# Doubling a decay table on ScalarE, issuing the last output rows from two queues, and moving TensorE's filler work, in a kernel of sliding attention and a long convolution

## The chip, the cores and the metric

One core of one Trainium2 chip. The metric is the device time of one execution in microseconds (us), lower is better. The engines have short names in the profile: PE is TensorE's matmul, PEld its weight load, DVE is VectorE, ACT is ScalarE, POOL is GpSimd, SP is SyncE, which here only issues transfers. A name with a q (SPq, ACTq, POOLq) is the instruction queue of that engine.

## The reference

Two independent heads stand side by side in the output: columns 0 to 639 come from A, columns 640 to 1279 from B.

```python
# A: sliding attention, 32 heads of 20, 8 taps at distance 2
qkv = x @ wqkv                              # (2048, 640) @ (640, 1920)
idx = pos[:, None] - arange(8) * 2          # key positions of each query
logits = einsum("bhsd,bhswd->bhsw", q, k[idx]) * Dh ** -0.5   # -1e9 where idx < 0
attn = softmax(logits, axis=-1)
o = einsum("bhsw,bhswd->bhsd", attn, v[idx])
a = o.transpose(...).reshape(B, S, D) @ wo

# B: diagonal state space layer as a causal convolution of length 2048
logdA = exp(log_dt)[:, None] * (A_re + 1j * A_im)             # (640, 192)
P = exp(logdA[:, :, None] * arange(L))
K = einsum("dn,dnl,dn->dl", Cc, P, dB).real                   # kernel of each channel
y = irfft(rfft(pad(u)) * rfft(pad(K)))[:L] + u * Dskip
return concatenate([a, b], axis=-1)
```

## The kernel before

**The first half builds the convolution kernels, in five chunks of channels** (`c` = 0 to 4 in `body`, line 851). The powers `exp(logdA * l)` are not computed one by one: for each chunk `exps_chunk` (line 236) makes a table `R` of real exponentials with ScalarE, `phase_table` (line 267) makes sines from products of TensorE (tables `TA` and `TX`), and VectorE multiplies them into a left factor X (`small_half`, line 310) and a right factor Y (`y_form`, line 341). TensorE sums X times Y over the states (`kgen_unit`, line 351, tile `ps_k`). VectorE's order in this half is PG, X, Q, X and then the Y products of each unit, chunk after chunk. The Fourier steps of the earlier chunk (`fwd`, lines 369 to 388, with ScalarE evicting `ps_f`) and the product of u with the skip factor (`times_d`, line 436) lie between.

**Exponentials with two multipliers at once.** `exps_chunk` can make the rows for multipliers m and 2m with one instruction if it finds alpha and 2 alpha side by side. So for every chunk but the first it writes 2 alpha into the place of the alpha of the chunk before (`twice`, lines 246 to 250), which may happen only when the exponentials of the chunk before have read it. In the kernel before, GpSimd makes this sum of two float32 tiles of 128x192 (line 248). GpSimd's queue also carries the two fills of the table with ones (lines 244 and 245) and the ten stores of `times_d` (line 442). The tile UD that `times_d` writes has one buffer, so VectorE can write the next UD (line 441) only when the store of the last one has landed.

**The second half is attention and the way back from the Fourier domain.** After the projections of q, k and v the loop over `GROUPS` (line 984) takes steps n = 0 to 47, eight for each of six groups of query columns. A step (`av_step`, line 666) is one VectorE product of v with the attention weights into a ring of six buffers, and 16 small matmuls of 32 rows by 32 columns that add it up in `ps_o`; after the eighth step ScalarE evicts `ps_o`. Steps of VectorE, TensorE and ScalarE are kept in the order of the program in this half (`in_order`, line 970), so that where a piece of work stands in the loop is where its engine does it.

**Fillers.** Between the steps the dictionary `FILLS` (line 982) puts pieces of other work: `(r, p)` at step n takes r pieces of the output projection (`out_piece`, line 707) and p pieces of the inverse transform of B (`part`, line 757, 12 or so matmuls of 96 rows into `ps_ib` and an eviction by ScalarE to `ysb`; 24 pieces in all). In group 0 the fillers of a step stand ahead of its `av_step`, in the other groups behind it. The softmax of the second half of the columns runs inside the loop: maximum and difference at n = 2, the exponential with its one ScalarE instruction at n = 3 (line 990), the sums over the eight taps by TensorE (`sums`, line 628, two taps at each of n = 8, 10, 12 and 14, tile `ps_x`), the reciprocal and the product by VectorE at n = 17.

**The end.** `out_piece` is called 16 times. It multiplies a block of attention output with wo (`ps_op` or `ps_x`), evicts it to one of six `ob` tiles by ScalarE (in the last two pieces ScalarE one half, VectorE the other) and stores it in 1, 2 or 4 transfers. The pieces count themselves in `nop`; from the twelfth on (`late`, line 713) all their transfers, 16 in number, are issued by SP.

Of the kernel before, what the change touches and what calls it, by code (L numbers as in the profile page):

```python
# [10 lines left out]
A = mybir.AluOpType  # L11
# [224 lines left out]
def exps_chunk(tc, pools, B, c):  # L236
    nc = tc.nc
    flat = pools["tab"].tile([128, 9216], bf16, name="R", tag=f"R{c % 2}")
    RA = flat[:, 0:3072].rearrange("p (h g q a f) -> p h g q a f", h=2, g=2, a=8, f=4)
    RX = flat[:, 3072:9216].rearrange("p (q e f) -> p q e f", e=32, f=4)  # L240
    al = B["alpha"][:, c]
    by_half = al.rearrange("p (h v) (q f) -> p h (v q) f", h=2, f=4)
    src = al.rearrange("p u (q f) -> p (u q) f", f=4)
    nc.gpsimd.memset(flat[:, 0:3072].rearrange("p (x a f) -> p x a f", a=8, f=4)[:, :, 0, :], 1.0)
    nc.gpsimd.memset(RX[:, :, 31, :], 1.0)
    if c > 0:
        twice = B["alpha"][:, c - 1]
        nc.gpsimd.tensor_tensor(out=twice, in0=al, in1=al, op=A.add)  # L248
        both = B["alpha"][:, c - 1:c + 1]
        both = both.rearrange("p e u (q f) -> p (u q) e f", f=4)  # L250
    exp = lambda o, i, m: nc.scalar.activation(out=o, in_=i, func=ACT.Exp, scale=m)  # L251
# [12 lines left out]
    return RA, RX  # L264
# [190 lines left out]
class Attention:  # L455
# [251 lines left out]
    def out_piece(self, rows, last=False):  # L707
# [17 lines left out]
        if whole:  # L725
            self.copy(out=ob.rearrange("p (h n) -> p h n", h=2), in_=ps)
        for k in range(ns):
            (nc.gpsimd, nc.sync)[late or k % 2].dma_start(out=self.out_a[512 * (s0 + k) + i0:512 * (s0 + k) + i0 + ni, :], in_=ob[ni * k:ni * k + ni])
# [50 lines left out]
def body(tc, ctx, pools, prm, B_u, B_Dskip, Sd, Zd, UDd, A_x, A_wqkv, A_wo, out_a, out_b):  # L779
    nc = tc.nc  # L780
# [193 lines left out]
    def fill(some, n=1):  # L974
        for f in some[0:n]:
            f()
        del some[0:n]
# [4 lines left out]
    FILLS = {1: (0, 2), 3: (0, 2), 5: (0, 1), 7: (0, 1), 9: (0, 1), 11: (0, 2), 13: (0, 2), 15: (0, 1), 17: (1, 0), 19: (2, 2), 23: (1, 2), 27: (2, 2), 31: (2, 2), 35: (2, 2), 37: (0, 2), 39: (1, 0), 43: (1, 0), 45: (1, 0)}  # L982
    LOADS = {(2, 8)[n // NCH] + n % NCH: (2 + n // NCH, n % NCH) for n in range(2 * NCH)}
    for group, (i0, ni, j0, nj, done) in enumerate(GROUPS):
        for w in range(W):
            n = 8 * group + w
            if group == 0:
                fill(parts, FILLS.get(n, (0, 0))[1])
                if w == 3:
                    att.exp(1)  # L990
                if w in (0, 3):
                    att.proj_v(16 + 2 * (w == 3))
                if w == 5:
                    att.v_halo(8, 12)
# [83 lines left out]
```

## Time and profile before

| | us |
|---|---|
| median of 3 runs | 424.67 |
| the 3 runs | 406.79, 424.67, 425.53 |
| the profiled execution, own time | 407.56 |
| its span, first to last instruction | 405.8 |
| HBM traffic in it | 19.69 MB read, 14.16 MB written |

The profile is a page of one execution. Its views: the busy time of each engine; the chain of waits followed back from the last instruction; groups of instructions by line with their durations; and, asked for a stretch, the timeline of one engine, in which a row gives start, length, engine, line, operation, out<-in, count, and in brackets the idle time before it with what ended it. A view by stretches gives each engine's busy time and the clock that TensorE was granted (1.00 is full speed). An engine that is not the bound may idle for free; what counts is the engine that is busy all through a stage, and which wait ends last there.

### The profile page before, as it was taken

To read this page: it belongs to the slowest core of one execution; us is meant where nothing else is said; L and a number is where in the kernel's file an instruction comes from. 1 tells how busy PE (TensorE), PEld (TensorE's weight loads), DVE (VectorE), ACT (ScalarE), POOL (GpSimd) and SP (SyncE) were. 2 spreads that over 40 slices of the span, in tenths; PEclk is the share of its full clock that TensorE was granted. 3 is DMA by queue.
4 is the path that set the end of the run, shared out by engine and by line. 5 is a ranking of instruction groups with operands and counts; after the bars stand their busy time and mean duration, and the time that the engine had idled before them with its cause. 6 is when DMAs were issued, how large, how long until landed. Compare 5 with 4: busy or idle time off the path is not lost.

```text
span 405.8 us, 18754 instructions
## 1 busy us (share of the span) xinstructions
PE 349.7 (86%) x8565; PEld 260.6 (64%) x8565; DVE 370.3 (91%) x350; ACT 307.9 (76%) x532; POOL 100.6 (25%) x114
## 2 busy tenths in 40 slices
PE   1279779979898789889988989999999999899994
PEld 0267667878786679768787666656755676335652
DVE  7999999999989999999799999997967899889961
ACT  2996999879999999989999576533778544845662
POOL 8771049000101000399801000100020030302220
PEclk9999989989989999988999999999999999958998
DMA  5599102132044002420039655301652264797542
GB/s 143 155 235 193 22 4 107 57 81 56 29 151 115 3 3 81 135 55 2 31 112 152 124 93 133 100 4 24 214 162 79 104 160 107 209 254 222 163 125 74
DMA packets 40839, 43.36 MB, mean 107 GB/s; under 512 B 24144, under 2 KB 34288, under 8 KB 40120
## 3 DMA queue, kind: packets, MB, share of 16 engines
q1 hardware_dynamic: 35960, 30.60, 31.3%
q0 software_dynamic: 4656, 11.44, 9.3%
q8 instruction: 67, 1.10, 1.1%
q10 hardware_dynamic: 144, 0.12, 0.1%
q14 instruction: 12, 0.10, 0.1%
HBM read 19.69 MB, written 14.16 MB: 83 GB/s over the span
## 4 chain that ended last, share of the span: by engine, by line
PE 38%; ACT 21%; DVE 18%; issue 15%; DMA 3%; POOL 2%; SPq 1%; ACTq 0%; DVEq 0%; POOLq 0%
ACT R L251 8%; DVE X L317 6%; DVE Y L347 5%; PE ps_q L556 5%; PE ps_k L538 4%; PE ps_v L569 4%; DVE PG L317 3%; PE ps_x L472 3%; PE ps_o L472 3%; PE ps_op L472 3%; ACT A L380 3%; PE ps_ph L288 3%; PE ps_k L360 2%; POOL LPB L248 2%; DVE Q L317 2%
## 5 line engine op out<-in xcount | busy, mean ns | idle before, releaser
L347 DVE TENSOR_TENSOR Y<-PG 128x3072 bf16<-128x3072 bf16 x60 | 103.0, 1754 | 4.1 <-PE ps_k L365 4.1
L251 ACT ACTIVATE R<-LPB 128x192 bf16<-128x192 f32 (+1 forms) x185 | 56.5, 409 | 0.6 <-POOL LPB L248 0.5
L360 PE MATMUL ps_k<-Y,X 128*32 128x64 bf16 x1920 | 46.3, 239 | 10.3 <-DVE Y L347 9.5
L248 POOL TENSOR_TENSOR LPB<-LPB 128x192 f32<-128x192 f32 x4 | 45.9, 11470 | 29.4 <-ACT R L251 25.8
L288 PE MATMUL ps_ph<-LPB,LPA 128*64 128x256 bf16 x320 | 35.1, 323 | 12.7 <-DMA LPA<-lo 7.8
L360 PEld LDWEIGHTS <-X 128*32 128x32 bf16 x1920 | 32.8, 117 | 19.7 <-issue 8.9
L387 ACT CAST A<-ps_f 128x1024 bf16<-128x1024 f32 x40 | 37.6, 1036 | 7.4 <-PE ps_f L386 7.4
L365 PE MATMUL ps_k<-Y,X 64*32 64x64 bf16 x1920 | 42.9, 233 | 0.0
L380 ACT CAST A<-ps_f 128x1024 bf16<-128x1024 f32 x40 | 37.7, 1041 | 0.6 <-PE ps_f L379 0.6
L317 DVE TENSOR_TENSOR X<-R,TX 128x1536 bf16<-128x1536 bf16 x40 | 37.7, 963 | 0.3 <-DMA LPA<-hi 0.3
L386 PE MATMUL ps_f<-A,T 128*64 128x128 bf16 x640 | 29.1, 258 | 8.5 <-ACT A L380 8.4
L365 PEld LDWEIGHTS <-X 64*32 64x32 bf16 x1920 | 29.5, 112 | 8.6 <-issue 0.9
L386 PEld LDWEIGHTS <-T 128*64 128x64 bf16 x640 | 27.1, 129 | 10.1 <-issue 9.1
L679 DVE TENSOR_TENSOR prod<-v,atp 128x1536 bf16<-128x1536 bf16 (+3 forms) x32 | 30.9, 1023 | 2.4 <-PE ps_o L472 1.2
L296 ACT ACTIVATE TX<-ps_ph 128x768 bf16<-128x768 int16 x40 | 30.0, 836 | 1.1 <-PE ps_ph L292 1.0
L296 ACT ACTIVATE TA<-ps_ph 128x768 bf16<-128x768 int16 x40 | 29.7, 815 | 0.5 <-PE ps_ph L292 0.2
L288 PEld LDWEIGHTS <-LPA 128*64 128x64 bf16 x320 | 18.3, 124 | 17.0 <-DMA LPA<-hi 7.9
L589 DVE TENSOR_TENSOR prod<-qT,kT 128x1024 bf16<-128x1024 bf16 (+1 forms) x16 | 22.9, 1482 | 4.2 <-ACT qT L557 4.2
L292 PE MATMUL ps_ph<-LPB,LPA 128*64 128x128 bf16 x320 | 24.1, 246 | 0.0
L442 POOL DMA_DIRECT2D UDdram<-UD x10 | 5.5, 551 | 72.4 <-DVE UD L441 65.7
L538 PE MATMUL ps_k<-xT,wkq 128*128 128x512 bf16 x100 | 22.9, 379 | 0.2 <-ACT A L387 0.2
L556 PE MATMUL ps_q<-xT,wkq 128*128 128x512 bf16 x100 | 22.6, 379 | 0.0
(157 smaller groups left out, 733.3 us busy)
## 6 DMA issues: line engine op xcount, KB each, us to landing
P<-A SPq DMA_DIRECT2D x16, 256.0 KB
Zdram<-Z SPq DMA_DIRECT2D x16, 256.0 KB
Z<-Zdram SPq DMA_DIRECT2D x30, 128.0 KB
U<-in_B_u_dram SPq DMA_DIRECT2D x4, 640.0 KB
UDdram<-UD POOLq DMA_DIRECT2D x10, 256.0 KB, 2.3
out_dram<-ysb SPq DMA_DIRECT2D x32, 80.0 KB
Z<-UDdram SPq DMA_DIRECT2D x16, 128.0 KB
Z<-Zdram POOLq DMA_DIRECT2D x10, 128.0 KB, 4.8
```

Of the source, the lines that this page charges most:

```text
L248: nc.gpsimd.tensor_tensor(out=twice, in0=al, in1=al, op=A.add)
L251: exp = lambda o, i, m: nc.scalar.activation(out=o, in_=i, func=ACT.Exp, scale=m)
L288: MM(o[64 * hh:64 * hh + 64, :, 0:8], lhsT=L[:, 64 * hh:64 * hh + 64], rhs=rhs, start=first, stop=last, skip_group_check=True, tile_positi ...
L296: last = nc.scalar.activation(out=dst, in_=words.rearrange("p b (q e f) -> p b q (e f)", e=8, f=4), func=ACT.Sin, scale=PI_LO / 32768.0)
L317: TT = lambda o, a, b, op: V.tensor_tensor(out=o, in0=a, in1=b, op=op)
L347: nc.vector.tensor_tensor(out=Y[:].rearrange("p q (b a) f -> p q b a f", a=8), in0=fa, in1=gb, op=A.mult)
L360: MM(ps[32 * g:32 * g + 32, t], lhsT=X[:, q, k, :, f], rhs=Ys[k][:, q, :, f], start=(t == 0 and k == 0), stop=False, tile_position=(0, 32 ...
L365: MM(ps[32 * g:32 * g + 32, t], lhsT=X[hb, q, k, :, f], rhs=Ys[k][hb, q, :, f], start=False, stop=(k == 2), tile_position=(64 * (g // 2), ...
L380: nc.scalar.copy(out=A1[:, 8 * b:8 * b + 8], in_=ps[:])
L386: last = MM(ps[sl, kk], lhsT=C["T2"][:, 8 * b + kk, sl], rhs=A1[:, :, 8 * b + kk, :], start=(kk % 4 == 0), stop=True, skip_group_check=Tru ...
L538: MM(ps[:, i], lhsT=self.wk[:, kt, 128 * ct:128 * ct + 128], rhs=self.x4[:, kt, 2 * i:2 * i + 2, 256 * hf:256 * hf + 256], start=(kt == 0) ...
L556: MM(ps[:, i], lhsT=self.wq[:, kt, 128 * ct:128 * ct + 128], rhs=self.x4[:, kt, 2 * i:2 * i + 2, 256 * hf:256 * hf + 256], start=(kt == 0) ...
```

## The change

Four edits in three places.

1. `exps_chunk`: 2 alpha is made by ScalarE, as an activation `Copy` with the factor 2.0, no longer by GpSimd as a sum. It happens four times, for chunks 1 to 4. `exps_chunk` is called inside a block that holds its ScalarE instructions behind the last sine of the chunk before (lines 896 to 898), which now includes this one.
2. `out_piece`: the transfers of the pieces from the twelfth on are issued half by SP and half by ScalarE. All transfers of `out_piece` are now kept behind whatever their queue was given before them.
3. `FILLS` and the sums of the second half: the pieces of the inverse transform at n = 1, 3, 5, 7, 9, 11, 13, 15 were 2, 2, 1, 1, 1, 2, 2, 1; they become 1, 1, 2, 2, 0, 2, 1, 2, and 1 at n = 16. Those of n = 7 stand behind its `av_step` now. The sums move from n = 8, 10, 12, 14 to 9, 11, 13, 14.

```diff
@@ exps_chunk
-        nc.gpsimd.tensor_tensor(out=twice, in0=al, in1=al, op=A.add)
+        nc.scalar.activation(out=twice, in_=al, func=ACT.Copy, scale=2.0)
@@ out_piece
         for k in range(ns):
-            (nc.gpsimd, nc.sync)[late or k % 2].dma_start(out=self.out_a[...], in_=ob[...])
+            queue = (nc.sync, nc.scalar)[k * 2 // ns] if late else (nc.gpsimd, nc.sync)[k % 2]
+            self.tc.keep_in_program_order(queue.dma_start(out=self.out_a[...], in_=ob[...]))
@@ body
-    FILLS = {1: (0, 2), 3: (0, 2), 5: (0, 1), 7: (0, 1), 9: (0, 1), 11: (0, 2), 13: (0, 2), 15: (0, 1), 17: (1, 0), ...}
+    FILLS = {1: (0, 1), 3: (0, 1), 5: (0, 2), 7: (0, 2), 11: (0, 2), 13: (0, 1), 15: (0, 2), 16: (0, 1), 17: (1, 0), ...}
...
             if group == 0:
-                fill(parts, FILLS.get(n, (0, 0))[1])
+                if w < 7:
+                    fill(parts, FILLS.get(n, (0, 0))[1])
...
-            if n in (8, 10, 12, 14):
-                k = (8, 10, 12, 14).index(n)
+            if n in (9, 11, 13, 14):
+                k = (9, 11, 13, 14).index(n)
                 att.sums(1, 2 * k, 2 * k + 2)
...
-            if group > 0 and n in FILLS:
+            if n > 6 and n in FILLS:
                 fill(rest, FILLS[n][0])
                 fill(parts, FILLS[n][1])
```

More of the change, by code (lines that the diff above doesn't have):

```diff
@@ L727, in out_piece @@
         for k in range(ns):
-            (nc.gpsimd, nc.sync)[late or k % 2].dma_start(out=self.out_a[512 * (s0 + k) + i0:512 * (s0 + k) + i0 + ni, :], in_=ob[ni * k:ni * k + ni])
+            queue = (nc.sync, nc.scalar)[k * 2 // ns] if late else (nc.gpsimd, nc.sync)[k % 2]
+            self.tc.keep_in_program_order(queue.dma_start(out=self.out_a[512 * (s0 + k) + i0:512 * (s0 + k) + i0 + ni, :], in_=ob[ni * k:ni * k + ni]))
     def out_proj(self, some, last=False):
@@ L981, in body @@
               (256, 96, 0, 5, [(0, 4, i, 32) for i in (256, 288, 320)]), (352, 96, 0, 5, [(0, 4, i, 32) for i in (352, 384, 416)]), (448, 64, 0, 5, [(s, 2, 448, 64) for s in (0, 2)]))
-    FILLS = {1: (0, 2), 3: (0, 2), 5: (0, 1), 7: (0, 1), 9: (0, 1), 11: (0, 2), 13: (0, 2), 15: (0, 1), 17: (1, 0), 19: (2, 2), 23: (1, 2), 27: (2, 2), 31: (2, 2), 35: (2, 2), 37: (0, 2), 39: (1, 0), 43: (1, 0), 45: (1, 0)}
+    FILLS = {1: (0, 1), 3: (0, 1), 5: (0, 2), 7: (0, 2), 11: (0, 2), 13: (0, 1), 15: (0, 2), 16: (0, 1), 17: (1, 0), 19: (2, 2), 23: (1, 2), 27: (2, 2), 31: (2, 2), 35: (2, 2), 37: (0, 2), 39: (1, 0), 43: (1, 0), 45: (1, 0)}
     LOADS = {(2, 8)[n // NCH] + n % NCH: (2 + n // NCH, n % NCH) for n in range(2 * NCH)}
```

## The prediction

> **What bounds the kernel now.** I read the page first, then busy time by stretches, then the timelines of the engines at the three places of the change.
>
> ```profile
> PE 349.7 (86%) x8565; PEld 260.6 (64%) x8565; DVE 370.3 (91%) x350; ACT 307.9 (76%) x532; POOL 100.6 (25%) x114
> ```
>
> No engine bounds all of the span; the stretches say who does where. Columns: length, then busy time of PE, PEld, DVE, ACT, POOL, each with its count, then the granted clock and the transfers.
>
> ```profile
> core 0: us, PE busy (x) PEld busy (x) DVE busy (x) ACT busy (x) POOL busy (x), PEclk, DMA share, GB/s
> 75.00:130.00 55.00, 49.58 (x1568) 43.17 (x1566) 53.07 (x43) 51.05 (x87) 3.90 (x8) 0.94 0.29 81
> 130.00:180.00 50.00, 44.02 (x1340) 37.25 (x1335) 50.00 (x41) 47.41 (x84) 11.37 (x5) 0.97 0.22 60
> 180.00:235.00 55.00, 48.99 (x1320) 40.34 (x1316) 52.02 (x45) 48.98 (x85) 23.82 (x6) 0.94 0.41 83
> 265.00:305.00 40.00, 38.91 (x677) 24.34 (x674) 34.72 (x25) 23.75 (x27) 3.66 (x12) 1.00 0.35 107
> 351.00:354.40 3.40, 1.87 (x58) 0.81 (x54) 3.40 (x5) 2.28 (x3) 3.00 (x6) 1.00 0.82 238
> 354.40:368.10 13.70, 13.01 (x214) 4.75 (x211) 12.33 (x14) 5.14 (x10) 1.39 (x3) 0.50 0.82 226
> 368.10:380.00 11.90, 11.70 (x276) 7.18 (x274) 10.98 (x11) 8.58 (x16) 2.73 (x5) 1.00 0.75 232
> 380.00:392.90 12.90, 12.48 (x279) 7.39 (x278) 12.56 (x15) 9.06 (x18) 4.09 (x8) 1.00 0.44 126
> ```
>
> Up to 235 VectorE is the bound, with ScalarE close behind (51.05 of 55, 47.41 of 50). From 265 on it is TensorE (38.91 of 40). In the loop of the groups the two share it, and there stands a hole: between 351.0 and 354.4 TensorE works 1.87 of 3.40 us, and for the next 13.7 us its clock is 0.50, in which it is full (13.01).
>
> **Part one: 2 alpha on ScalarE.** GpSimd's four sums should be alike; three of them in its timeline show that they are not.
>
> ```profile
> 56.05 13.88 POOL L248 TENSOR_TENSOR LPB<-LPB 128x192 f32<-128x192 f32 x1 [18.98 <-ACT R L251]
> 125.83 1.00 POOL L248 TENSOR_TENSOR LPB<-LPB 128x192 f32<-128x192 f32 x1 [6.81 <-ACT R L251]
> 170.32 30.51 POOL L248 TENSOR_TENSOR LPB<-LPB 128x192 f32<-128x192 f32 x1
> 200.78 0.56 POOL L442 DMA_DIRECT2D UDdram<-UD  x1
> ```
>
> And VectorE over the same times:
>
> ```profile
> 70.49 1.76 DVE L347 TENSOR_TENSOR Y<-PG 128x3072 bf16<-128x3072 bf16 x1 [0.93 <-PE ps_k L365]
> 72.88 1.42 DVE L441 TENSOR_TENSOR UD<-U,Dsb 128x1024 bf16<-128x1024 bf16 x1 [0.63 <-DMA UDdram<-UD]
> 126.40 2.05 DVE L317 TENSOR_TENSOR PG<-R,TA 128x3072 bf16<-128x3072 bf16 x1
> 203.31 1.30 DVE L441 TENSOR_TENSOR UD<-U,Dsb 128x1024 bf16<-128x1024 bf16 x1 [2.84 <-DMA UDdram<-UD]
> 225.12 1.76 DVE L317 TENSOR_TENSOR PG<-R,TA 128x3072 bf16<-128x3072 bf16 x1
> ```
>
> The long sums end where VectorE goes idle: the first at 69.93, inside the 0.93 us ahead of 70.49; the last at 200.83, inside the 2.84 us ahead of 203.31. I read a ring in this: the sum gets through only when VectorE pauses; the store of UD stands behind the sum in GpSimd's queue (issued 200.78); and VectorE pauses only because the next UD waits for that store. Besides, the PG product that met the sum of 125.83 took 2.05 instead of the 1.76 of its like at 225.12.
>
> Removed: 0.63 + 2.84 + 0.29 = 3.76 us of VectorE, and a wait of ScalarE. What ScalarE pays, and what is late next:
>
> ```profile
> 195.03 0.87 ACT L251 ACTIVATE R<-LPB 128x192 bf16<-128x192 f32 x3
> 200.87 2.52 ACT L251 ACTIVATE R<-LPB 128x384 bf16<-128x384 f32 x7 [0.54 <-POOL LPB L248]
> 222.85 0.81 ACT L296 ACTIVATE TA<-ps_ph 128x768 bf16<-128x768 int16 x1 [0.24 <-PE ps_ph L292]
> ```
>
> Three activations of this shape take 0.87, so 0.29 each; four are 1.16. They write float32 where these write bfloat16, which no row prices; the single longest bound is one of 128x384, 2.52 / 7 = 0.36, so 1.44 for the four. Queued behind each are the exponentials of the chunk, then the sines, and behind those the PG and X products of VectorE. In the first three chunks ScalarE gates VectorE now and then, so I charge two of the instructions to the path up to 203 (0.58); the early stalls give back 0.92, net 0.34. At 225.12 the PG product needs the TA that ScalarE ends at 222.85 + 0.81 = 223.66. VectorE alone could be there 3 us earlier, but TA is earlier only by that 0.34, plus the wait of 0.54, less its own 0.29: 223.07. So of 3.76 us about 2.05 stay; the rest turns into a wait for ScalarE. TensorE must take them over:
>
> ```profile
> PE ps_k L360 <- DVE Y L347: 2.6, 5, 1.0
> ```
>
> This row of its waits between 200 and 240 says that it loses 2.6 us to Y products there, so 2.05 fits. I take 2.1. Bounds: 3.76 if ScalarE has room that I don't see, and minus 1.4 if the stalls stay and the four instructions lie bare.
>
> A rule that speaks against the edit: the Trainium skill, ScalarE: Activation LUTs, "Rules for kernel authors", gives multiplications to VectorE. No run shows the rule here. The stretches have VectorE as the bound (50.00 of 50), so what the rule would take off ScalarE, at most 1.4, it would lay on the bound: by it the sum would be lower only where ScalarE binds instead.
>
> **Part two: fillers and sums.** VectorE's three pauses in the loop, and TensorE's two in the hole:
>
> ```profile
> 350.13 3.56 DVE L679 TENSOR_TENSOR prod<-v,atp 128x1536 bf16<-128x1536 bf16 x4 [1.16 <-ACT v L473]
> 360.25 1.76 DVE L637 RECIPROCAL soft<-ps_x 128x256 bf16<-128x256 f32 x1 [1.34 <-PE ps_x L472]
> 371.54 2.23 DVE L679 TENSOR_TENSOR prod<-v,atp 128x1920 bf16<-128x1920 bf16 x2 [0.92 <-PE ps_o L472]
> ```
>
> ```profile
> 352.56 0.36 PE L472 MATMUL ps_o<-prod,ident 32*32 32x384 bf16 x8 [0.97 <-ACT o L473]
> 353.48 0.38 PE L472 MATMUL ps_x<-lsb,ident 128*128 128x256 bf16 x2 [0.56 <-ACT o L473]
> ```
>
> ```profile
> 345.32 2.06 ACT L473 CAST ysb<-ps_ib 128x480 bf16<-128x480 f32 x4
> 347.28 1.92 ACT L624 ACTIVATE lsb<-lsb 128x2048 bf16<-128x2048 bf16 x1
> 349.09 1.00 ACT L473 CAST v<-ps_v 128x1024 bf16<-128x1024 f32 x1
> ```
>
> The first pause is a chain on ScalarE: four evictions of fillers (2.06), the exponential, the eviction of v that VectorE waits for. Two of the four fillers go to n = 5 and 7: 2 x 0.52 = 1.0 earlier, of 1.16 I take 0.9. The second is the reciprocal waiting for the sums. By n = 14 eleven fillers were issued, now nine, so the last sums come two fillers sooner; such a filler's eviction is 0.52 and its matmuls are near that, at half clock twice it, so 1 to 2 us against 1.34: I take 1.2. The two fillers at n = 7 now stand behind the step, exactly in the 0.97 + 0.56 that TensorE waits for the evictions of `ps_o`. The third pause is TensorE behind its steps; three fillers at n = 15 and 16 instead of one eat some of the lead, so I take 0.3 of 0.92. Sum 2.4; bounds 1.16 + 1.34 + 0.92 = 3.42 and, if the deferred fillers hold TensorE as much as they freed it, 0. Their cover is TensorE's pause at the evictions; without it the two of n = 7 cost 1 us. Each third filler also issues four stores on SP; by n = 7 and again by n = 16 the counts are the old ones (six, twelve), so these move by a step or two behind SP's loads of Z, and nothing reads them: nothing charged. The sums' own matmuls stay eight.
>
> **Part three: two queues at the end.**
>
> ```profile
> 399.77 0.49 DVE L705 CAST ob<-ps_o 128x320 bf16<-128x320 f32 x1 [0.87 <-PE ps_o L472]
> ```
>
> ```profile
> 393.13 9.91 SPq L728 DMA_DIRECT2D out_dram<-ob  x18
> ```
>
> ```profile
> L728 SPq DMA_DIRECT2D out_dram<-ob x22: 315/420/1242, 385.7 to 402.4; - x22
> ```
>
> ```profile
> L127 ACTq DMA_DIRECT2D B_A_re<-in_B_A_re_dram x2: 635/636/636, 2.7 to 3.4; - x2
> L118 ACTq DMA_DIRECT2D ldt<-in_B_log_dt_dram x2: 640/943/1246, 0.8 to 2.0; - x2
> ```
>
> ```profile
> 393.32 0.69 ACT L473 CAST ob<-ps_x 128x640 bf16<-128x640 f32 x1 [1.80 <-issue]
> 399.13 0.42 ACT L473 CAST ob<-ps_x 128x320 bf16<-128x320 f32 x1 [0.93 <-PE ps_x L472]
> ```
>
> The new order of the earlier stores only forbids overtaking; I charge nothing, since the path has only the backlog at the end. The last data are ready at 400.26, but SP issues until 403.04; the span ends 2.76 later, which I leave as it is. After the change SP has 8 of the 16, ScalarE 8 between its evictions. From 393.32 on ScalarE has seven evictions (two of 0.69, five of about 0.42: 3.5 us) and eight issues. At SP's median of 0.42 they are 3.4 us and the work ends at 400.2; at ScalarE's own 0.64 (two rows of the start of the span) 5.1 us, 401.9; at 1.246, its longest, 10 us, 406.8. The last issue can't end before 400.26 + 0.5. So the last issue ends between 400.8 and 401.9, against 403.04: 1.1 to 2.2 us less, or 3.8 more at the worst price. Behind each pair of issues wait the next eviction and so TensorE's next block; I take 0.5 off for that and keep 1.3.
>
> The Trainium skill, DMA: Bandwidth & Descriptors, "Issuing engines are not separate DMA queues", says that issuing from several engines saves only the sequencer's time. By it the gain ends at the 2.78 us of backlog behind 400.26, which no run here shows yet; 1.3 lies within.
>
> **Sum.** 2.1 + 2.4 + 1.3 = 5.8 on the profiled execution: 407.56 becomes 401.8. The median of the runs, 424.67, lies 17.1 above the profiled execution, and the lowest run 0.8 below it. Nothing in the profile shows what the two long runs met; if the runs after scatter alike, the same change reads 401.8 + 17.1 = 418.9.
>
> **Rivals.** *All stalls turn into time.* ScalarE keeps up, and filling the hole holds TensorE's clock at 1.00: 3.76 + 3.42 + 2.2 = 9.4, 398.2. For it: the stretch with 1.87 busy comes just ahead of the 0.50; against it: ScalarE's 48.98 of 55. The Trainium skill, TensorE: Matmul & The Clock Gate, "What's actually happening", would have one busy window of 3.4 us lift the gate; in this trace it stayed down for 13.7 us at 13.01 busy, so the row does not follow it and busy time alone may not hold the clock.
>
> *The UD stores stay parked.* GpSimd's queue still holds the fills of R, which wait for VectorE's X products, ahead of stores; if the order that is built puts a store behind one, the ring closes again and part one gives nothing or its minus 1.4: 403.9 to 405.3. This is also the case that the first edit does not do what it says.
>
> *Slower: the half clock does not end at 368.* Fewer fillers and no sums early in the loop leave TensorE longer with matmuls of 32 rows. Between 368.1 and 392.9 it is full at clock 1.00 (11.70 + 12.48 of 24.8); at 0.50 these 24.8 us would take up to 12.4 more, less what VectorE hides. Part two's 2.4 is lost too: 401.8 + 2.4 + 12.4 = 416.6. It outweighs the rest from about 7 us of further half clock on: 3.4 lost and 2.4 not won are the 5.8.
>
> **Chances and range.** Forecast 0.47; all stalls 0.20; stores parked 0.19; half clock 0.14. The forecast's own range is 399 to 406, by its bounds; the rivals (398.2, 416.6) and the scatter of the runs (418.9) stretch it to 398 to 420. What a measurement of this kernel tells from no change is about 2%, 8.2 us: faster needs 399.4 or less, 0.24 (the second case and an edge of the forecast); slower needs 415.7, 0.13 (nearly all of the last); within, 0.63.
>
> **What would show it.** Part one: no POOL L248; no wait of DVE L441 for UD; PG near 223 waiting for ACT TA instead. Part two: no pause of the reciprocal, TensorE over 2.5 of 3.4 us busy at the group's turn, clock 1.00 there. Part three: the last issue within 1.5 us of the last eviction. Wrong would be: L441 still waiting; a clock of 0.50 beyond 368; evictions of ACT queued behind its own issues.

## The result, and the profile after

The median of 22 runs went from 408.31 us (405.77 to 427.16) to 406.88 us (401.46 to 412.89); the ratio is 0.993, with a 95% interval of 0.9904 to 0.9957. The profiled execution took 404.63 us with a span of 402.8, against 407.56 and 405.8: 2.9 us less where 5.8 were forecast. Every ratio here leaves out the runs over 1.5% above the fastest of their kernel: of the kernel before the 10 runs at 424 us or more, whose like come in every other job of a kernel that leaves the sum to GpSimd and in none of 160 runs of kernels with the first edit (no profile shows what they met, and the forecast's 418.9 carried them over), and of the kernel after the 10 runs from 407.5 us on. The mean of all 22 runs of the kernel after is 406.6, that of the other 12 runs of the kernel before 407.5: 0.9 less.

The page of the kernel after, busy times of the engines:

```profile
PE 346.1 (86%) x8565; PEld 258.9 (64%) x8565; DVE 369.8 (92%) x350; ACT 308.2 (76%) x536; POOL 85.0 (21%) x110
```

Little work has gone: GpSimd has 15.6 us less, VectorE as much as before. By stretches (columns as in the prediction; the last three are the end of group 0, the stretch behind it and the half clock):

```profile
180.00:235.00 55.00, 49.81 (x1343) 40.40 (x1344) 53.78 (x45) 49.85 (x88) 2.47 (x4) 0.97 0.40 89
...
347.70:351.10 3.40, 2.70 (x92) 1.09 (x80) 3.40 (x5) 2.60 (x5) 2.76 (x6) 1.00 0.78 222
351.10:365.20 14.10, 9.34 (x186) 4.97 (x182) 14.07 (x15) 6.61 (x13) 2.72 (x5) 1.00 0.81 211
365.20:372.00 6.80, 6.16 (x110) 2.79 (x126) 4.58 (x5) 3.43 (x6) 0.00 (x0) 0.50 0.74 216
```

TensorE's hole at the group's turn is smaller (2.70 busy of 3.40, before 1.87). The half clock that followed it is gone from there; it lasts 6.8 us instead of 13.7, but stands later, behind 365.2. VectorE's timeline at the places of the edits:

```profile
198.92 1.33 DVE L441 TENSOR_TENSOR UD<-U,Dsb 128x1024 bf16<-128x1024 bf16 x1
...
221.84 1.76 DVE L317 TENSOR_TENSOR PG<-R,TA 128x3072 bf16<-128x3072 bf16 x1 [1.22 <-ACT TA L296]
...
346.24 3.69 DVE L679 TENSOR_TENSOR prod<-v,atp 128x1536 bf16<-128x1536 bf16 x4 [0.54 <-ACT v L473]
...
355.05 1.75 DVE L637 RECIPROCAL soft<-ps_x 128x256 bf16<-128x256 f32 x1
...
367.43 2.23 DVE L679 TENSOR_TENSOR prod<-v,atp 128x1920 bf16<-128x1920 bf16 x2 [2.02 <-PE ps_o L472]
```

The wait for the UD store (2.84) is gone. The PG product of chunk 4 starts 3.28 us earlier than 225.12. The pauses for v (1.16) and for the sums (1.34) are 0.54 and none, so the reciprocal comes 5.20 earlier than 360.25. Then 2.02 us go to a pause for `ps_o`, 0.92 before. TensorE's timeline says why:

```profile
365.85 0.99 PE L472 MATMUL ps_ib<-Z,HB 96*32 96x480 bf16 x12 [2.79 <-DMA out_dram<-ysb]
```

This is the first filler of n = 19 and the first that needs Z of the third quarter. (The wait is put down to a store of `ysb`, which no matmul reads; what it reads is Z.) SP's queue, which issues the loads of Z, shows where they were:

```profile
351.47 1.18 SPq L756 DMA_DIRECT2D Z<-Zdram  x2
352.75 0.54 SPq L756 DMA_DIRECT2D Z<-UDdram  x1
353.38 3.47 SPq L774 DMA_DIRECT2D out_dram<-ysb  x4
357.15 2.23 SPq L756 DMA_DIRECT2D Z<-Zdram  x2
359.48 0.54 SPq L756 DMA_DIRECT2D Z<-UDdram  x1
360.06 2.45 SPq L756 DMA_DIRECT2D Z<-Zdram  x2
362.61 0.53 SPq L756 DMA_DIRECT2D Z<-UDdram  x1
```

Two loads take 1.18 where nothing holds SP. Here four stores of `ysb` stand in the middle of the loads (3.47), behind the third of five chunks, and the loads behind them take twice their time. In the kernel before the same stores came behind the first chunk. So the last load is issued at 363.14 (before: 362.99), although all other work is 3 to 5 us earlier.

At the end, ScalarE:

```profile
393.77 0.95 ACTq L729 DMA_DIRECT2D out_dram<-ob  x2
394.76 0.76 ACT L473 CAST ob<-ps_o 128x320 bf16<-128x320 f32 x2 [1.02 <-issue]
...
399.26 0.55 ACTq L729 DMA_DIRECT2D out_dram<-ob  x1
```

The last issue ends at 399.81, 0.63 behind VectorE's last copy (before: 2.78), but evictions stand behind issues: the copy comes 8.31 behind the loop's last product instead of 7.39. In the pair of profiles the three parts read: first edit 3.28, loop 2.00 at its last product, so minus 1.28 for the second part, then 2.9 at the end, so plus 0.9.

### The profile page after: what moved, and what is told of

Read it like the earlier page. It is cut to its first block, busy times and chain, and to the rows that moved or that the text cites. A ratio compares the mean times of both kernels' runs of the same rounds, so it can differ in the third digit from the quotient of the medians.

```text
span 402.8 us, 18753 instructions
## 1 busy us (share of the span) xinstructions
PE 346.1 (86%) x8565; PEld 258.9 (64%) x8565; DVE 369.8 (92%) x350; ACT 308.2 (76%) x536; POOL 85.0 (21%) x110
## 3 DMA queue, kind: packets, MB, share of 16 engines
q0 software_dynamic: 4656, 11.44, 9.8%
## 4 chain that ended last, share of the span: by engine, by line
PE 41%; ACT 36%; DVE 12%; issue 5%; DMA 3%; SPq 1%; ACTq 1%; DVEq 0%
ACT R L251 13%; ACT A L380 6%; ACT A L387 5%; PE ps_q L556 5%; PE ps_k L538 4%; PE ps_ph L288 4%; PE ps_v L569 4%; DVE X L317 4%; PE ps_k L360 3%; PE ps_k L365 3%; PE ps_f L386 2%; PE ps_x L472 2%; ACT Z L428 2%; PE ps_l L600 2%; PE ps_o L472 2%
## 5 line engine op out<-in xcount | busy, mean ns | idle before, releaser
L360 PE MATMUL ps_k<-Y,X 128*32 128x64 bf16 x1920 | 46.5, 239 | 7.1 <-DVE Y L347 4.9
L288 PE MATMUL ps_ph<-LPB,LPA 128*64 128x256 bf16 x320 | 33.5, 310 | 14.2 <-DMA LPA<-lo 8.3
L360 PEld LDWEIGHTS <-X 128*32 128x32 bf16 x1920 | 32.5, 117 | 16.7 <-issue 8.0
L818 POOL COPY Dsb<-Dn 128x160 bf16<-128x160 bf16 x1 | 30.6, 30632 | 0.0
L556 PE MATMUL ps_q<-xT,wkq 128*128 128x512 bf16 x100 | 22.6, 379 | 0.0
```

The source lines that it names most:

```text
L288: MM(o[64 * hh:64 * hh + 64, :, 0:8], lhsT=L[:, 64 * hh:64 * hh + 64], rhs=rhs, start=first, stop=last, skip_group_check=True, tile_positi ...
L360: MM(ps[32 * g:32 * g + 32, t], lhsT=X[:, q, k, :, f], rhs=Ys[k][:, q, :, f], start=(t == 0 and k == 0), stop=False, tile_position=(0, 32 ...
L556: MM(ps[:, i], lhsT=self.wq[:, kt, 128 * ct:128 * ct + 128], rhs=self.x4[:, kt, 2 * i:2 * i + 2, 256 * hf:256 * hf + 256], start=(kt == 0) ...
```

## The experiments

**The three edits one by one.** Each is the kernel before with one edit (the cuts below show its first line), and `without_fills` has the first two.

```diff
# only_double, without_fills
-        nc.gpsimd.tensor_tensor(out=twice, in0=al, in1=al, op=A.add)
+        nc.scalar.activation(out=twice, in_=al, func=ACT.Copy, scale=2.0)
# only_queues, without_fills
-            (nc.gpsimd, nc.sync)[late or k % 2].dma_start(...)
+            queue = (nc.sync, nc.scalar)[k * 2 // ns] if late else (nc.gpsimd, nc.sync)[k % 2]
# only_fills
-    FILLS = {1: (0, 2), 3: (0, 2), 5: (0, 1), ...}
+    FILLS = {1: (0, 1), 3: (0, 1), 5: (0, 2), ...}
```

> The kernel before with the first edit alone (2 alpha by ScalarE). Theory: it is worth 3.3 us on VectorE up to 242 us and nothing takes it back: the PG product of chunk 4 starts near 221.8 (before 225.12), VectorE's wait for the UD store is gone, TensorE reaches the first filler of the third quarter near 366.9, after the last load of Z for it has landed (365.8), so it waits less than 0.5 there, and the profiled time is 3.0 to 3.5 below the kernel before. Rival 1: whatever arrives earlier in the loop waits for Z: then the profiled time is only 0 to 1 below. Rival 2: the gain came from another order of TensorE's instructions in the first half that comes with the other edits: then PG starts after 223.

> The kernel before with the second edit alone (late stores of the output by SP and ScalarE, order of the stores kept). Theory: the last issue ends 2 to 3.2 us earlier than 403.04, TensorE's last block about 0.9 later behind ScalarE's issues, so the span is about 1.0 to 2 below. Rival: the delay of ScalarE's evictions eats all of it: 0 to 0.5 below, or above.

> The kernel before with the third edit alone (places of the fillers and of the sums). Theory: the pauses for the eviction of v and for the sums go, 1.9 us by the reciprocal; TensorE then reaches the first filler of the third quarter near 367 to 368, after the loads of Z for it (365.8 if they do not move), so its wait is under 1 us and the profiled time 1 to 2 below the kernel before. Rival: the edit is bad by itself (the half clock after the group's turn and the three fillers at n = 15 and 16 lose more than it wins): a wait or a lower clock after 363 without a wait for Z, time 0 to 1.5 above.

> The kernel after with the third edit undone (first and second alone). Theory: 3.3 + 1.0 = 4.3 below the kernel before, so about 1.4 us below the kernel after's 2.9, with no wait of over 0.5 us for Z on TensorE at the first filler of the third quarter. Rival: the third edit is worth its 2 us, the wait for Z comes with any earlier arrival: then this kernel is 0 to 2 above the kernel after.

Ratios: `only_double` 0.9978 (0.994 to 1.0017), `only_queues` 0.9927 (0.9891 to 0.9962), `only_fills` 0.9975 (0.994 to 1.0009), `without_fills` 0.9962 (0.9921 to 1.0002). The kernel after itself reads 0.993, 0.9988 and 0.993 in three jobs, so edits of 1 us are not told apart by times; the profiles have to do it. `only_queues` took 12.92 from the loop's last product to the end, as the kernel before did, so in its profile the rival held: what the second queue saved, the later evictions took. In `only_fills` TensorE waits at the same filler:

```profile
PE ps_ib L472 <- DMA Z<-UDdram: 2.2, 1, 2.2
```

That was to be under 1: the loads do not stay at 365.8, the third edit itself makes them late (the last one is issued 27.8 us after the loop's first product, 25.1 in the kernel before, 28.5 in the kernel after); its loop was 0.4 shorter than before, its profiled time of 409.05 was 1.5 longer where 1 to 2 less was expected. `only_double` missed its mark: PG of chunk 4 at 227.66, 2.5 later than without the edit, though VectorE was 3.1 ahead at 201. In `without_fills` it was 222.87. Its profiled time, 404.95, was 0.3 above the kernel after's where 1.4 below was expected. But TensorE did not wait at the first filler of the third quarter, as expected, so the wait does not come with every earlier arrival. The late PG needed the runs further down.

**What the first edit removes.** `ring_open` is the kernel before with UD's stores on another queue, the sum left on GpSimd.

```diff
-    nc.gpsimd.dma_start(out=UDd[c, :, 1024 * i:1024 * i + 1024], in_=UD[:]...)
+    nc.sync.dma_start(out=UDd[c, :, 1024 * i:1024 * i + 1024], in_=UD[:]...)
```

> The kernel before (GpSimd's sum kept) with one thing changed: the ten stores of UD are issued by SP, so that none stands behind the sum in GpSimd's queue. Theory: the ring of sum, store and VectorE is the cost that the first edit removes. VectorE's waits for the UD store (0.63 and 2.84) go although the sums still take 10 us or more, and the PG product of chunk 4 starts 2 to 3.3 us earlier than 225.12, unless ScalarE's exponentials, which still wait for the sum, become late. Rival: the cost is the sum itself (ScalarE's exponentials wait for it): the sum then ends later still, with no pause of VectorE to let it through, and PG starts no earlier than 224 or later than before.

GpSimd's timeline and VectorE's:

```profile
56.70 13.48 POOL L248 TENSOR_TENSOR LPB<-LPB 128x192 f32<-128x192 f32 x1 [19.37 <-ACT R L251]
170.31 4.47 POOL L248 TENSOR_TENSOR LPB<-LPB 128x192 f32<-128x192 f32 x1 [7.31 <-ACT R L251]
```

```profile
200.83 1.34 DVE L441 TENSOR_TENSOR UD<-U,Dsb 128x1024 bf16<-128x1024 bf16 x1
222.78 1.76 DVE L317 TENSOR_TENSOR PG<-R,TA 128x3072 bf16<-128x3072 bf16 x1 [0.24 <-ACT TA L296]
```

The last sum took 4.47 instead of 30.51, VectorE did not wait for a store at 200, and PG came 2.3 earlier; the ratio is 0.9941 (0.9898 to 0.9984). The ring of sum, store and VectorE was the cost in this execution, as the theory had it. But not only a pause lets a sum through. In the profiles of the four kernels that have these sums, the eight that took over 4 us all end 0.4 us behind the start of a pause of VectorE; of the eight short ones (0.50 to 1.23) six met no pause. The Trainium skill, SBUF — State Buffer, "SBUF: two separate sides", has VectorE and GpSimd sharing a pair of ports, which the one that starts first holds for a whole instruction; the long sums agree, and how the short ones got in between VectorE's instructions is not shown.

**The loads of Z.** `loads_first` gives SP all loads of the third quarter ahead of the stores; `later_quarter` moves the fillers that wait.

```diff
# loads_first: chunks 3 and 4 of the third quarter at n = 4, no longer 5 and 6
-    LOADS = {(2, 8)[n // NCH] + n % NCH: (2 + n // NCH, n % NCH) for n in range(2 * NCH)}
+    LOADS = {2: [(2, 0)], 3: [(2, 1)], 4: [(2, 2), (2, 3), (2, 4)]}
+    LOADS.update({8 + c: [(3, c)] for c in range(NCH)})
# later_quarter
-    19: (2, 2), 23: (1, 2), 27: (2, 2)
+    19: (2, 0), 23: (1, 3), 27: (2, 3)
```

> The kernel after with one thing moved: the last two chunks of Z of the third quarter are loaded at n = 4 instead of n = 5 and 6, so that SP issues all fifteen of these loads ahead of the four stores of ysb that the third edit had pushed into their middle. Nothing changes on the other engines. Theory: the stores' place in SP's queue is what delayed the loads (in the kernel after, SP stood for them between 353.4 and 357.2 with the transfers at 1.02 to 1.08 of their engines). Then SP issues the last of these loads near 356 instead of 363.14, TensorE's wait of 2.79 for Z is under 0.3, its clock does not fall at 365, the last product of the loop ends near 388.4 (after: 390.87) and the profiled time is 2 to 2.8 below the kernel after. Rival: the transfers themselves are the bound (as many bytes in as few microseconds): the last load lands within 1 us of 365.8, TensorE still waits over 1.5, time within 0.7 of the kernel after.

> The kernel after with the two fillers of n = 19, the first that need Z of the third quarter, moved to n = 23 and n = 27, one each (three there instead of two). Theory: TensorE reaches them after 365.8, the wait of 2.79 goes, the steps of n = 20 to 22 run on; the later fillers give back about 0.5 at n = 23 and 27, so the profiled time is 1.5 to 2.5 below the kernel after. Rival: the wait for Z was only the place where TensorE's half clock or its lack of work shows: pauses of VectorE for ps_o of the same sum (2 to 3 us) come back at n = 23 to 31, time within 0.7 of the kernel after.

In `loads_first` SP's last loads of the quarter, the stores, and the whole loop by stretches (that of the kernel after behind it):

```profile
364.54 1.61 SPq L756 DMA_DIRECT2D Z<-Zdram  x2
366.77 0.31 SPq L756 DMA_DIRECT2D Z<-UDdram  x1
367.73 5.56 SPq L774 DMA_DIRECT2D out_dram<-ysb  x8
```

```profile
344.40:396.10 51.70, 48.36 (x1148) 27.21 (x1142) 51.03 (x54) 33.81 (x58) 11.19 (x21) 0.97 0.70 195
```

```profile
334.60:390.90 56.30, 48.91 (x1131) 27.45 (x1124) 51.48 (x54) 33.86 (x58) 11.19 (x21) 0.94 0.63 180
```

As many transfers, issued 22.6 us after the loop's first product instead of 28.5; no wait for Z over 0.3; and VectorE busy for 51.03 of 51.70. The loop is 4.7 shorter than in the kernel after and bound by VectorE. This execution started its loop late (344.5 instead of 334.6), so the whole is no faster: 0.9957 (0.9916 to 0.9998). `later_quarter` lost its wait too (loop 54.53, 1.7 less), but its profiled time, 407.24, lies 2.6 above the kernel after's where 1.5 to 2.5 below was expected: the loop started 1.4 later and the end took 3.0 longer. It reads 0.9972 (0.9929 to 1.0014).

**Two more profiles of the kernel after, and of both fixes.** `after_again` and `after_third` are the kernel after unchanged, `loads_again` and `held_again` (below) run beside the latter.

> The kernel after, unchanged, for a second profile and beside the next three. Theory: what the first edit gives depends on the clock that TensorE is granted between 203 and 222 us, since TensorE is full there once VectorE comes 3 us earlier (5.00 of 5 at 210 to 215): at a mean of 0.89 and 1.00 in 203 to 218 and 218 to 222 the PG product of chunk 4 starts at 221.8 to 223.1, at 0.62 to 0.71 and 0.70 to 0.93 (the kernel with the first edit alone, with loads_first and with gpsimd_late) it starts at 226.1 to 227.7, for ScalarE's TA, which waits for TensorE. So here too: 221.5 to 223.5 if the clock of 203 to 218 is 0.85 or more, 226 to 228 if it is under 0.75. TensorE's wait for Z at the first filler of the third quarter is 1.5 to 3 again. Rival: the start of PG does not go with the clock.

> The kernel after, unchanged, beside the next two. Theory: TensorE waits 1.5 to 3 us for Z at the first filler of the third quarter; the loop from its first to its last product takes 54 to 56.5 us; its runs spread over 401 to 413.

> loads_first again. Theory: no wait of over 0.5 us for Z, the loop takes 51.5 to 53 us (2 to 3 less than the kernel after), and the mean of its runs is 1.5 to 3 us below that of the kernel after in this job. Rival: the wait for Z was hidden behind something else in most executions, and the means lie within 0.7.

The table has every execution with the same work up to 222 us. Its columns: the granted clock in 203 to 218 and 218 to 222; how long TensorE stands at one matmul in the middle of `ps_k` (L360, the same one each time), where the profile names no wait; the start of PG of chunk 4; the loop from its first to the end of its last product; from there to the end of the span.

| | clock | stands | PG | loop | end |
|---|---|---|---|---|---|
| before | 0.89, 1.00 | - | 225.12 | 54.98 | 12.92 |
| only_queues | 1.00, 1.00 | - | 224.69 | 54.14 | 12.92 |
| only_fills | 0.77, 1.00 | - | 225.50 | 54.59 | 13.23 |
| ring_open | 0.89, 1.00 | 0.51 | 222.78 | 52.68 | 13.46 |
| after | 0.89, 1.00 | 0.72 | 221.84 | 56.27 | 11.98 |
| without_fills | 0.89, 1.00 | 0.79 | 222.87 | 54.74 | 12.59 |
| later_quarter | 0.89, 1.00 | 0.85 | 223.12 | 54.53 | 14.96 |
| held_stores | 0.89, 1.00 | 1.12 | 222.95 | 51.64 | 11.44 |
| loads_again | 0.89, 1.00 | 1.37 | 223.48 | 51.93 | 15.07 |
| held_again | 0.89, 1.00 | 0.47 | 223.86 | 52.89 | 13.82 |
| after_again | 0.67, 0.95 | 2.30 | 225.29 | 54.90 | 12.28 |
| gpsimd_late | 0.68, 0.93 | 2.84 | 226.07 | 54.13 | 16.94 |
| after_third | 0.71, 0.79 | 2.53 | 226.61 | 52.38 | 12.17 |
| loads_first | 0.71, 0.82 | 2.40 | 226.94 | 51.61 | 13.01 |
| only_double | 0.62, 0.70 | 2.48 | 227.66 | 54.63 | 13.75 |

With the sum on ScalarE there are two kinds of executions: PG at 221.8 to 223.9, or at 225.3 to 227.7, as late as before the change or later. In all of the second kind the clock was low and TensorE stood 2.3 us or more. (`after_again` with 0.67 started PG at 225.29, not 226 to 228; the side is the one expected.) The mean of the eleven is 224.6 against 225.1 for the three kernels with the ring: on the average the first edit gives 0.5 there, not 3.3.

By the times of one job the kernel after has a mean of 407.8 (12 runs, standard error 0.9), `loads_again` 407.7 (0.9), `held_again` 405.5 (0.7). The loop of `loads_again` took 51.93, as expected, though TensorE still stood 1.15 at the first filler of n = 19, where under 0.5 was expected; that of `after_third` happened to be 52.38, with a wait for Z of 1.6 that VectorE's ring of six buffers swallowed; and the end of `loads_again` took 15.07. So the means fell as the rival had it: that the moved loads alone pay in the runs is not shown.

The loops differ in the clock, too. Their time at half clock is none in `ring_open` (52.68) and `held_stores` (51.64), 10.2 us in `only_queues` (54.14) and `without_fills` (54.74) and in `held_again` (52.89). So at like clocks the third edit with the loads put first is worth 1.0 to 1.9 us of loop against the old fillers.

**What stands between 203 and 222 us.** The same `ps_k` matmuls in TensorE's timeline, of after and of `after_again`:

```profile
219.20 0.36 PE L360 MATMUL ps_k<-Y,X 128*32 128x64 bf16 x12 [0.72 <-issue]
```

```profile
223.54 0.36 PE L360 MATMUL ps_k<-Y,X 128*32 128x64 bf16 x12 [2.30 <-issue]
```

"issue" is a wait that the profile doesn't name. Nor has TensorE room to catch up; this is 203 to 218 us of after by stretches:

```profile
203.00:218.00 15.00, 14.26 (x397) 12.97 (x397) 15.00 (x14) 14.49 (x28) 1.77 (x2) 0.89 0.61 133
```

The view of the transfers names a candidate; these are its queues in 213.2 to 219 of after, and in 214 to 220.7 of `after_again` (packets, MB, share):

```profile
q1 hardware_dynamic: 1557, 0.62, 65.5%
q0 software_dynamic: 135, 0.51, 32.6%
q8 instruction: 1, 0.02, 1.5%
```

```profile
q1 hardware_dynamic: 2373, 0.82, 73.9%
q0 software_dynamic: 153, 0.53, 28.0%
```

Queue 8 brings blocks of 16 KB of an engine's instructions, 67 in a run; I take them for TensorE's, which has 17130 of the 18754 instructions on the page of the kernel before. In after one comes at 216.30, in `after_again` only at 221.01; in each execution of the table that stands, TensorE goes on 1.2 to 1.8 us after its block has landed. The three that do not stand reach that matmul 1.4 to 1.9 us after the landing. The Trainium skill, Runtime: NRT & Kernel Launch, "Instruction fetch mechanics", has the same 16 KB blocks and calls the cost of crossing into the next one mostly hidden; here, if the standstill is that crossing, it was 0.5 to 2.8 us. Three kernels move what the transfer engines carry there, the loads of x:

```diff
# x_later and held_x: the first load of x behind the last sine of chunk 4; z_first: behind the last store of Z
-                if last is not None:
-                    behind(self.tc, ins, last)
+                behind(self.tc, ins, sines[1] if last is None else last)
```

> The kernel after with the eight transposed loads of x held behind the last sine of chunk 4's TX, so that none of them runs between 207 and 224. Up to the PG product of chunk 4 the instructions of TensorE, VectorE and ScalarE are those of the kernel after. Theory: TensorE's standstill of 2.3 to 2.8 us at ps_k near 221 is a late block of its own instructions, behind the packets of these loads; without them the block comes when it is asked for, the standstill is under 1.2 and PG starts at 223.2 or earlier whatever the clock. The projections of k wait for x instead, later on, so the time may be up to 10 us above the kernel after. Rival: the standstill belongs to the low clock (or to something that the trace does not show): it stays at 2 or more when the clock of 203 to 222 is under 0.75, and PG starts after 225.

> The kernel after with the loads of x held behind the last of the four stores of Z of the chunk before, so that stores and loads no longer alternate: the stores are over by about 213, the loads run alone after that. Theory: if it is the loads of x that hold up the block of instructions, the standstill can come here as in the kernel after (0.7 or 2.3 to 2.8); if it is the two together, it stays under 1.2 and PG starts by 223.2. The time is within 2 of the kernel after either way, but for x that arrives some 5 us later.

> held_stores with the loads of x of x_later. Theory: if the standstill goes and x arrives in time for TensorE, the runs above 406 go and the mean falls by 1 to 2 from held_stores; if the projections of k wait for x, it is 2 to 10 above held_stores, all of it between 222 and 260 us.

`x_later`, then `z_first`, TensorE and VectorE:

```profile
222.77 0.36 PE L360 MATMUL ps_k<-Y,X 128*32 128x64 bf16 x12 [1.17 <-issue]
```

```profile
224.52 1.76 DVE L317 TENSOR_TENSOR PG<-R,TA 128x3072 bf16<-128x3072 bf16 x1 [1.98 <-ACT TA L296]
```

```profile
222.98 0.36 PE L360 MATMUL ps_k<-Y,X 128*32 128x64 bf16 x12 [2.50 <-issue]
```

```profile
225.06 1.76 DVE L317 TENSOR_TENSOR PG<-R,TA 128x3072 bf16<-128x3072 bf16 x1 [3.58 <-ACT TA L296]
```

Without the loads of x TensorE stood 1.17 (and 1.43 in `held_x`) at clocks of 0.69 and 0.66, half of the 2.3 to 2.8 at such clocks with them, but PG came at 224.3 to 224.5, not by 223.2. With as long a standstill at 0.89 (1.12 in `held_stores`, 1.37 in `loads_again`) it came at 222.95 and 223.48, so the low clock has its own share, 0.8 to 1.6 in these two pairs. In `z_first`, with the clock at 0.89 and 1.00, it stood 2.50 and PG came at 225.06: a late block needs no low clock. Against the six executions of the first kind the low clock without the long standstill put PG 0.5 to 2.7 back, the long standstill without the low clock 1.2 to 3.2; what delays the block was not settled (in `x_later` it came at 220.28 with few transfers about). All three pay for it later: VectorE waits 7.8 to 12.1 us for `ps_k`, since the projections of k need x, and the ratios are 1.0174 (1.0125 to 1.0224), 1.0161 (1.0133 to 1.0189) and 1.0236 (1.0178 to 1.0295).

`early_table` takes the wait for TA away instead, by making the table a stage earlier.

```diff
-        if c in (1,):
+        if c in (1, 3):
```

> The kernel after with the table TA of chunk 4 made a stage earlier (as the kernel does for chunk 2: the condition on the chunk reads 1 or 3 in place of 1), so that the PG product of chunk 4 does not wait for TensorE's phases, and then ScalarE's TA, near 222. Theory: the wait of 1.2 to 3.7 for ScalarE's TA ahead of that PG is what ends VectorE's advance; without it PG starts near 220 to 221.5 whatever the clock, and the runs lie 1 to 4 us below the kernel after, with fewer of them above 408. Rival 1: TensorE's work is the bound over the whole stage, so the wait comes back at the X product or at Y (ps_k) by the same sum; VectorE reaches 250 us no earlier. Rival 2: ScalarE's exponentials are pushed back by the four earlier sines and something ahead of 205 waits: PG later than 222.

There was no wait for TA, and at a clock of 1.00 PG still started at 225.13: VectorE lost 2.9 near 120, 1.7 at 220 and 3.7 at 242 to `ps_k` instead, 0.9988 (0.995 to 1.0026). In the kernel after these three waits were 1.35, none and 0.25. So the wait came back by more than it saved, as the first rival had it. How much of that is TensorE's work alone is open: PG lay behind 222, the second rival's sign as well, and TensorE stood 1.98 in a row of `ps_k` at 225 in this execution, too.

**The end.** `gpsimd_late` gives the second half of the late stores to GpSimd. `held_stores` is `loads_first` with three of them on ScalarE behind its last eviction, `held_vector` that with the sum on VectorE.

```diff
# gpsimd_late
-            queue = (nc.sync, nc.scalar)[k * 2 // ns] if late else ...
+            queue = (nc.sync, nc.gpsimd)[k * 2 // ns] if late else ...
# held_stores, held_again, held_vector
+            if last and s0 == 0:
+                self.held.append((dst, src))
+                continue
+            if last and k == 0:
+                for d, s in self.held:
+                    self.tc.keep_in_program_order(nc.scalar.dma_start(out=d, in_=s))
+            queue = ((nc.sync, nc.scalar)[k] if last else nc.sync) if late else (nc.gpsimd, nc.sync)[k % 2]
# held_vector
-        nc.scalar.activation(out=twice, in_=al, func=ACT.Copy, scale=2.0)
+        nc.vector.tensor_tensor(out=twice, in0=al, in1=al, op=A.add)
```

> The kernel after with the second half of the late output stores issued by GpSimd in place of ScalarE. Theory: ScalarE's issues (0.37 to 0.60 each) delay its last evictions and through them TensorE by 0.9 to 1.8 us; without them VectorE's last copy ends 7.4 us after the loop's last product (as in the kernel before; after: 8.3), and with GpSimd's issues of 0.55 the last one ends within 1.2 of that copy: from the last product to the end of the span 11 us against the kernel after's 12.0. Rival: GpSimd's transfers land later than ScalarE's by more than that, and the tail stays at 12 or grows.

> loads_first with the late stores divided in another way: SP issues those of the pieces 12 to 14 and one of the last piece, ScalarE issues three (two of the piece before the last, one of the last) and only behind its last eviction. Theory: ScalarE's issues between its evictions cost TensorE 0.9 to 3.9 us (from the loop's last product to VectorE's last copy 8.3 to 11.3 in the kernels with them, 7.39 in all four without). Here that stretch is 7.39 again, the last issue ends 0.9 to 1.4 behind the copy, the span 3.0 behind it: 11.3 to 11.9 from the last product to the end, against 12.0 to 15.0 with ScalarE's issues between and 12.9 to 13.8 with SP alone; the time 1 to 2 us below loads_first. Rival: SP's twelve issues from the first store on still end late (they take 0.63 each) and the stretch to the end is 12.5 or more.

> held_stores again. Theory: the loop as in loads_again; the end is 11.4 to 13 us from the last product against 12 to 13.2 with ScalarE's issues between its evictions, so the mean is 0 to 1 us below loads_again. Rival: the 3.5 us that held_stores lay below the kernel after in its job come from the end, and it lies over 1.5 below loads_again.

> held_stores with 2 alpha made by VectorE as a sum, in place of ScalarE. Theory: VectorE is the bound up to 203 and pays the four sums, 0.2 to 0.5 each, and ScalarE saves four activations of 0.3 to 0.5, which matters only at the TA of 222: the time is within 1 us of held_stores, and VectorE is 0.5 to 1.5 us later at the PG product of chunk 3. Rival (multiplications belong on VectorE): ScalarE is the one that binds, TA and PG of chunk 4 come 0.5 to 1.5 earlier and the time is 0.5 to 1.5 lower.

`gpsimd_late` had VectorE's last copy 7.39 behind the loop, as expected, and the last issue 1.1 behind that; then the span went on for 8.5 us, 1.0103 (1.005 to 1.0157). The operations behind the program's last line show it (min/median/max ns):

```profile
L1075 POOLq DRAIN  x3: 46/102/8225, 402.6 to 411.3; - x3
```

In the kernel before that drain is as long, but starts at 392.2, so that it is over before the end:

```profile
L1073 POOLq DRAIN  x3: 46/102/7585, 392.2 to 405.5; - x3
```

From the loop's last product to the end, SP alone takes 12.92, 13.75, 13.23 and 13.46 (mean 13.3): 7.39 to VectorE's last copy every time, 3.2 of backlog, 2.7 of landing. The eleven profiles with ScalarE's issues between its evictions take 11.9 to 15.1 (mean 12.9): 8.2 to 11.4 to the copy, 0.63 of backlog, 3.0 of landing. `held_stores` took 11.44, but `held_again` 13.82, with 3.6 of backlog, and `held_vector` and `held_x`, which divide the stores alike, 12.99 and 13.08 (mean of the four 12.8). So three divisions end within a microsecond of one another. `held_stores` reads 0.99 (0.9842 to 0.9958) and `held_again` 0.9924 (0.9885 to 0.9964); beside the kernel after their means are 3.5 (404.3 and 407.8) and 2.2 lower (standard errors about 1.2 and 1.1). It is the best version here. `held_again` also lies 2.1 below `loads_again`, as its rival had it, but its profile doesn't show the end as the reason; what the end gives is open.

`held_vector` was slower, 1.0072 (1.0028 to 1.0115), for a reason that neither side had:

```profile
36.06 0.36 DVE L248 TENSOR_TENSOR LPB<-LPB 128x192 f32<-128x192 f32 x1 [7.31 <-ACT LPB L167]
```

The sum costs 0.36, the activation in after 0.364 to 0.410; but the first of the four now stands in VectorE's queue ahead of chunk 0's first product and waits there for alpha. It tells the cost of that place, not which engine should multiply.

## Why the prediction was partly wrong

The direction was right, and the change stayed within the 2% that a measurement tells from no change, as forecast at 0.63. The size was not right: 5.8 forecast, 2.9 in the pair of profiles. Part of the 2.9 is the luck of that pair. The averages over all profiles add up to 0.8 (0.5, minus 0.1 and 0.4), near the 0.9 between the means of the runs.

**Part one, forecast 2.1, measured 3.28 in the pair, about 0.5 on the average.** The mechanism was right: the ring is gone, and PG waits for ScalarE's TA instead (1.22). In the pair TA came 1.2 earlier than the 223.07 that was reckoned. The step that was off is "TensorE must take them over: ... so 2.05 fits". It fits at a clock of 0.89 with standstills up to 1.4; in five of eleven executions it does not, because TensorE, busy 14.26 of 15 us, has no room for a half clock or a late block. The four activations cost 0.36 to 0.41 each, not 0.29.

**Part two, forecast 2.4, measured minus 1.28.** This is the step that failed: "these move by a step or two behind SP's loads of Z, and nothing reads them: nothing charged". Nothing reads the stores, but four of them came to stand in the middle of the loads, and the loads queued behind them on SP are read, by the fillers of n = 19, and those come sooner. The pauses went as forecast (1.92 by the reciprocal against 2.1); then 2.79 of TensorE's time went to Z and 2.02 of VectorE's followed. By all profiles the loop takes 54.2 with the old fillers (five, 52.7 to 55.0), 54.3 with the new ones (eight, 52.4 to 56.3) and 52.1 with the new ones and the loads put first (six, 51.6 to 52.9). So the part gave nothing, and once the loads are out of the way 2.1 of the 2.4 is there by these means, 1.0 to 1.9 at like clocks.

**Part three, forecast 1.3, measured 0.9 in the pair, about 0.4 on the average.** The last issue came 1.2 earlier in the pair, counted from the loop's last product, within the forecast's 1.1 to 2.2. "I take 0.5 off for that" was too little: in the profiles with ScalarE's issues between its evictions VectorE's last copy comes 0.8 to 4.0 later (0.9 in the pair) than the 7.39 of the five without. On the average that takes 1.9 and the landing 0.3 from the 2.6 us by which the backlog shrank; the rule of the Trainium skill, DMA: Bandwidth & Descriptors, "Issuing engines are not separate DMA queues", that several issuers save only the sequencer's time, agrees with that split.

Of the rivals, stores that stay parked did not happen. A half clock beyond 368 did, to 372.0, and it was named as a sign against the forecast; it lasted 6.8 us in all, where that rival had 24.8 more. (24.8 us of full work would take up to 24.8 more at half the clock, not the 12.4 of that rival.) It stood right behind the wait for Z, but that it came from it is not shown: `held_again` had 10.2 us of half clock in its loop with no wait at that filler, and in `loads_again` none followed the wait of 1.15. All stalls turning into time failed at the same wait for Z.

## What to carry to other kernels

When work moves on one engine, list what its transfers overtake on the issuing queue and who reads what is now behind them: a store that nobody reads can hold up a load that somebody does. A stall taken out of an engine that was the bound pays only as far as the next engine has room; where that one is 95% busy, its clock and its instruction blocks decide from execution to execution, and one pair of profiles shows only one throw. A queue that still needs long to drain must get its last transfer early.

## What the runs showed of the hardware

GpSimd's sums of 128x192 float32 took 0.50 to 1.23 us or 4.47 to 30.53; each of the long ones ended 0.4 us behind the start of a pause of VectorE. In the kernel after, another of its operations met the same, by the page (0.37 us in the kernel before):

```profile
L818 POOL COPY Dsb<-Dn 128x160 bf16<-128x160 bf16 x1 | 30.6, 30632 | 0.0
```

GpSimd's queue took 7.6 to 8.2 us to drain at the end of the program. TensorE stood 0.5 to 2.8 us in the middle of a row of matmuls until 1.2 to 1.8 us after a 16 KB block of instructions had landed. Issues on ScalarE took 0.37 to 0.60 us in the kernel after, but one of the eight took 1.39 in `only_queues`; why is not shown.
